# Batch 0 of a linear-attention and MLP kernel: k's sums as rows, two denominators at once, numerators of two chunks in single banks

## The chip, the core and the metric

The kernel runs on one core of a Trainium2 chip. The core has five engines that work side by side and meet at semaphores: PE (TensorE, matmuls and transposes, with PEld for its weight loads), DVE (VectorE), ACT (ScalarE), POOL (GpSimd) and SP (SyncE, which here only starts transfers). Each engine takes its instructions strictly in the order in which the program gives them. Matmul results land in PSUM, which PE writes and VectorE and ScalarE read; a bank of it holds 512 fp32 values in each of 128 partitions. The metric is the device time of one launch in microseconds, as the median of several runs.

## What is computed

Linear attention with cosine weights, then a two-layer MLP, in fp32 at the borders:

```python
def phi(x, c, s):                      # c, s: cos and sin of pi/2 * position / S
    r = np.maximum(x, 0.0)
    return np.concatenate([r * c, r * s], axis=-1)
q_p, k_p = phi(q, cos_w, sin_w), phi(k, cos_w, sin_w)
kv  = np.einsum('bhsf,bhsd->bhfd', k_p, v)
z   = np.sum(k_p, axis=2)
num = np.einsum('bhsf,bhfd->bhsd', q_p, kv)
den = np.einsum('bhsf,bhf->bhs', q_p, z)[..., None] + 1e-06
x   = (num / den), heads side by side  # [B*S, H*D]
h   = x @ w_in
out = (h * (1.0 / (1.0 + np.exp(-1.702 * h)))) @ w_out
```

B = 8 batches, H = 8 heads, S = 576 positions, D = 64, so phi has 128 features; d_model = 512, d_ff = 2048.

## The kernel before, in words

Batches run one after the other. For each, k and q are turned into `kr` and `qn` (`trig`, L142 on VectorE or POOL and L140 on ScalarE), PE forms k^T v per pair of heads (`kv_mm`, L207), q is transposed into `qT` (features on partitions), numerators are `qT` times k^T v (`num_mm`, L230), VectorE divides them by the denominators (`num_div`, L254, after L236 and L238), the quotient `xn` is transposed into `x` (model dimension on partitions), and the MLP follows: `mm1` (L295) with its gelu on ScalarE (L300), `mm2` (L332) with its copy out (L336). In steady state the attention of the next batch is spread between the matmuls of `mm2`. A batch has 576 positions: four chunks of 128 and a tail of 64, and the tails of all batches go through the MLP together at the end (L312).

The order on every engine is written out by hand: the calls at the end of the kernel are the program order, there is no scheduler that moves them. Waits are put in where one engine reads what another writes, and where a buffer is used again. Two pools in PSUM matter. `pmm` has four buffers of one bank (named `mm`), `pat` two buffers of two banks (named `at`). A buffer is given out again in turn, and its next writer waits for the last reader of the tile before.

Batch 0 has nothing to hide behind, and its order (L355 to L435) is what the change touches:

- SP issues k in two parts (chunks 0 to 2, then 3 to 8, in pieces of 64 positions) and q in two parts (0 to 3, 4 to 8). POOL waits for k's first part through a one-element copy into `gate` (L130) and then issues v in two halves of two head pairs (`vb`) and the column groups 0 and 1 of W_in. After its own share of q (piece 8, L142) and a second `gate` copy that waits for v's second half (L383), it issues groups 2 and 3, and then the loads for batch 1 and W_out.
- PE begins with filler matmuls on a zeroed tile (`idle`, L346), then sums k over positions: `ksum` (L218) takes `kr` as the weights and a two-column selector `sel` as the moving operand, four matmuls of two columns for each of nine pieces, with one filler between pieces. The result has features on partitions, so VectorE copies it straight into column 64 of `kvs` (`ksum_evac`, L222). `kvs` holds k^T v and z side by side.
- `qturn_pe(c)` (L171) transposes the two 64-position pieces of chunk c, and `qevac(c)` copies them into `qT` (L181 on VectorE, L179 on ScalarE).
- `kv_mm(0, 2)` and `kv_mm(2, 4)` form k^T v for the two halves of the head pairs, `kv_evac` (L212) copies them into `kvs`.
- `den_early(0)` (L244) forms the denominators of chunk 0 alone, ahead of its numerators. For chunks 1 to 4 the denominator is column 64 of each head's numerator block, so `num_mm` writes 65 columns per head into a two-bank tile of `pat`.
- `xturn_mm(c)` (L274) transposes `xn` into columns of the same `pat` tile that the numerators leave free, `xturn_evac` (L280, ScalarE) copies it into x. The tail goes by a transposing transfer on SP (`xturn_dma`, L285).
- `part(c, fcs)` runs `mm1` for one chunk and one or more column blocks `fc` of W_in: four matmuls of 128 columns each (`mm1_part`, L295). The four blocks 0 to 3 are filled chunk by chunk in four banks, and then `gelu` runs on them and `mm1(0, 4)` begins, with 512 columns at a time.

Of the kernel before, what the change touches and what calls it, by code (L numbers as in the profile page):

```python
# [9 lines left out]
F32 = mybir.dt.float32  # L10
BF16 = mybir.dt.bfloat16
# [8 lines left out]
def kernel(  # L20
# [9 lines left out]
    nc = tc.nc  # L30
# [30 lines left out]
    for t, src, cut in ((kf, k, 192), (qf0, q, 256)):  # L61
# [10 lines left out]
    nc.gpsimd.memset(ident, 1.0)  # L72
    nc.gpsimd.affine_select(out=ident, in_=ident, compare_op=mybir.AluOpType.is_equal,
                            fill=0.0, base=0, pattern=[[-1, 128]], channel_multiplier=1)
    warm = const.tile([128, 512], BF16)
    nc.vector.memset(warm, 0.0)
    pos_f = const.tile([128, NP], F32)
    nc.vector.tensor_copy(pos_f, pos_i)
    nc.vector.tensor_scalar(pos_f[64:128, 0:NS], pos_f[64:128, 0:NS], float(-S), None, op0=ADD)
# [43 lines left out]
    def load_win(g):  # L123
        nc.gpsimd.dma_start(out=w_in_sb[g], in_=win_r[:, :, ts(g, 512)])
# [10 lines left out]
    def trig(dst, src, j, act=False, eng=nc.vector):  # L135
        i = src[:, :, ts(j, 64)]
        for cs, w in enumerate((cosw, sinw)):
            o = dst[:, j, :, ts(cs, 64)]
            if act:
                nc.scalar.activation(o, i, AF.Relu, scale=w[:, j:j + 1])  # L140
            else:
                eng.tensor_scalar(o, i, 0.0, w[:, j:j + 1], op0=MAX, op1=MUL)  # L142
# [21 lines left out]

    tps = {}

    def qturn_pe(c, home=None):
        tp = pmm.tile([128, 2, NI, 128], BF16, name="mm") if home is None else home
        for j in range(2 * c, min(2 * c + 2, NS)):
            for i in range(NI):  # L170
                nc.tensor.transpose(tp[:, j % 2, i], qn0[:, j, i, :], ident)  # L171
        tps[c] = tp

    def qevac(c, act=False):
        n = min(2 * c + 2, NS) - 2 * c
# [26 lines left out]
    def kv_mm(i0, i1, rhs, col, n):  # L202
        for i in range(i0, i1):
            for j in range(NS):
                for hh in range(2):
                    r = slice(hh * 64, hh * 64 + 64)
                    nc.tensor.matmul(st["kv", i][:, hh, ds(col, n)], kr[r, j, i, :], rhs(r, i, j),  # L207
                                     start=(j == 0), stop=(j == NS - 1))

    def kv_evac(i0, i1, n=65):  # L210
        o = st["kvs"][:, :, i0:i1, 0:n]
        nc.vector.tensor_copy(o, st["ps", i0].rearrange("p hh (i e) -> p hh i e", e=65)[:, :, :, 0:n])  # L212

    def ksum(j):
        if j == 0:
            st["z"] = pmm.tile([128, NI, 2], F32, name="mm")
        for i in range(NI):
            nc.tensor.matmul(st["z"][:, i], kr[:, j, i, :], sel, start=(j == 0 and i == 0),  # L218
                             stop=(j == NS - 1 and i == NI - 1))

    def ksum_evac():
        nc.vector.tensor_copy(st["kvs"][:, :, :, 64], st["z"].rearrange("f i hh -> f hh i"))  # L222
# [11 lines left out]
    def inv_of(d):  # L234
        den = small.tile([128, 2, 4], F32, name="den")
        nc.vector.tensor_scalar(den, d, 1e-6, None, op0=ADD)  # L236
        inv = small.tile([128, 2, 4], F32, name="inv")
        nc.vector.reciprocal(inv, den)  # L238
        return inv

    def den_early(c):
        d = pmm.tile([128, 2, 4], F32, name="mm")
        for h in range(H):
            nc.tensor.matmul(d[:, h // 4, h % 4:h % 4 + 1], qT[:, h, ts(c, 128)],  # L244
                             st["kvs"][:, h % 2, h // 2, 64:65], start=True, stop=True)
        return inv_of(d)

    def num_div(c, inv=None):
        ps = nums[c][0]
# [13 lines left out]
    def x_open(b):  # L263
        x[b] = xpool.tile([128, KC, MT], BF16, name="xT")
# [74 lines left out]
                eng = nc.sync if last else nc.gpsimd  # L339
                eng.dma_start(out=dst[:, c0:c1], in_=ysb[p0:p0 + n, c0:c1])  # L340

    def idle(n, w=None):
        if w is None:
            w = pmm.tile([128, 512], F32, name="mm")
        for _ in range(n):
            nc.tensor.matmul(w, warm[:, 0:128], warm, start=True, stop=True)  # L346
        return w

    def vb_rhs(r, i, j):
# [2 lines left out]
    def vt_rhs(r, i, j):  # L352
        return vt[r, j, i, 0:65]

    w = idle(12)  # L355
    for j in (0, 1):
        trig(kr, kf, j)
    for j in (2, 6, 7, 8):
# [2 lines left out]
        trig(kr, kf, j)  # L361
    kv_open(0, 2)
    kv_open(2, 4)
    for j in (0, 1, 2):
        ksum(j)
    for j in (3, 6, 4, 7, 5):
        idle(1, w)
        ksum(j)
    idle(1, w)
    ksum(8)  # L370
    for j in (0, 1):
        trig(qn0, qf0, j)
    ksum_evac()
    idle(1, w)
    qturn_pe(0)
    for j in (2, 3):
        trig(qn0, qf0, j, act=True)
    idle(2, w)
    qturn_pe(1)
    for j in (4, 5):  # L380
        trig(qn0, qf0, j)
    trig(qn0, qf0, 8, eng=nc.gpsimd)
    nc.gpsimd.tensor_copy(gate[0:1, 1:2], vb[0:1, 3, 0:1])  # L383
    load_win(2)
    load_win(3)
    kv_mm(0, 2, vb_rhs, 0, 64)
    qturn_pe(2)
    for j in (6, 7):
        trig(qn0, qf0, j, act=True)
    qevac(0)  # L390
    qevac(1)
    qevac(2, act=True)
    inv0 = den_early(0)
    kv_evac(0, 2, 64)
    kv_mm(2, 4, vb_rhs, 0, 64)
    kv_evac(2, 4, 64)
    qturn_pe(3)
    qevac(3, act=True)
    num_mm(0)
    num_div(0, inv0)  # L400
    num_mm(1)
    num_div(1)
    qturn_pe(4)
    qevac(4)
    idle(1)
    x_open(0)
    xturn_mm(0)
    xturn_evac(0, 0)
    num_mm(2)
    num_div(2)  # L410
    xturn_mm(1)
    xturn_evac(0, 1)

    def part(c, *fcs):
        for fc in fcs:
            mm1_part(0, fc, c * 128, c * 128 + 128)

    part(0, 0, 1, 2, 3)
    num_mm(3)
    num_div(3)  # L420
    xturn_mm(2)
    xturn_evac(0, 2)
    part(1, 0, 1, 2, 3)
    num_mm(4)
    num_div(4)
    xturn_mm(3)
    xturn_evac(0, 3)
    xturn_dma(0, 4)
    part(2, 0, 1, 2)
    part(3, 0, 1)  # L430
    part(2, 3)
    part(3, 2, 3)
# [150 lines left out]
```

## Time and profile before

| what | us |
|---|---|
| median of 3 runs | 291.59 (291.50 to 292.52) |
| the profiled execution | 292.75 |
| its span, first to last instruction | 291.0 |
| k's second part: first use on VectorE | 6.79 |
| q's second part: first use on VectorE | 10.67 |
| first matmul of k^T v | 11.38 |
| first matmul of W_in (chunk 0) | 16.97 |
| busy: PE, ACT, DVE, POOL | 281.8, 133.1, 123.7, 37.8 |

All times of instructions are from the profiled execution, counted from the start of its span. A group of the profile is a source line, an engine, an operation and its tiles; `PE at L230` in the chain of waits is a matmul of line 230 that writes a tile named `at`. In the timeline, a bracket behind a row tells how long the engine was idle before it and what ended that. Matmul rows are longer than the distance between their starts, because matmuls overlap in the array; where a sum goes by distances of starts, the text says so. Some matmul records are missing from a trace.

### The profile page before, as it was taken

How to read it: one execution, taken by the hardware profiler on the slowest of the kernel's cores; microseconds unless marked ns; L12 is line 12 of the kernel's file. 1: busy time of each engine (PE TensorE's matmuls, PEld its weight loads, DVE VectorE, ACT ScalarE, POOL GpSimd, SP SyncE). 2: the span in 40 equal slices, each digit the busy share in tenths (PEclk: the TensorE clock that was granted, in tenths of full speed). 3: DMA queues.
4: the chain of work that ended last, by engine and by line, in shares of the span. 5: the costliest groups of instructions: out<-in, count | busy, mean ns of one | idle time of the engine just before them, and what ended most of it. 6: DMA issues, size and time to landing. Idle time of an engine off the chain costs nothing.

```text
span 291.0 us, 5656 instructions
## 1 busy us (share of the span) xinstructions
PE 281.8 (97%) x2247; PEld 153.0 (53%) x2282; DVE 123.7 (43%) x356; ACT 133.1 (46%) x232; POOL 37.8 (13%) x71
## 2 busy tenths in 40 slices
PE   6989999999999999999999999999999999999995
PEld 2685475555555555555455545554555455544444
DVE  3872656912657354826582567156624200000000
ACT  6857564793157214721463136412651176751111
POOL 6560042301210011001100110011000100002000
PEclk9999999999999999999999999999999999999999
DMA  7999999982699877989797579846952600002322
GB/s 239 247 213 289 368 247 362 239 193 76 128 271 260 219 131 260 289 184 147 221 314 198 96 203 346 222 102 159 373 94 72 119 36 1 0 2 44 84 90 72
DMA packets 67770, 52.48 MB, mean 180 GB/s; under 512 B 47968, under 2 KB 57952, under 8 KB 67744
## 3 DMA queue, kind: packets, MB, share of 16 engines
q1 hardware_dynamic: 60320, 32.52, 47.0%
q0 software_dynamic: 7424, 19.60, 23.9%
q8 instruction: 18, 0.29, 0.4%
q14 instruction: 8, 0.07, 0.1%
HBM read 36.70 MB, written 9.44 MB: 159 GB/s over the span
## 4 chain that ended last, share of the span: by engine, by line
PE 91%; DMA 3%; ACT 2%; DVE 1%; issue 1%; SPq 1%; ACTq 0%
PE mm L332 42%; PE mm L295 37%; PE mm L312 5%; PE at L230 3%; PE at L207 3%; DMA qf<-in_q_dram 3%; ACT g L300 1%; PE at L274 1%; DVE qn L142 1%; DVE qT L181 0%; PE at L171 0%; ACT qT L179 0%; SPq L62 0%; DVE xn L254 0%; ACT xT L280 0%
## 5 line engine op out<-in xcount | busy, mean ns | idle before, releaser
L332 PE MATMUL mm<-w_out_sb,g 128*128 128x512 bf16 (+1 forms) x506 | 116.7, 372 | 1.3 <-issue 0.2
L295 PE MATMUL mm<-xT,w_in 128*128 128x512 bf16 (+1 forms) x551 | 111.9, 360 | 0.5
L300 ACT ACTIVATE g<-mm 128x512 bf16<-128x512 f32 x128 | 75.6, 598 | 31.0 <-PE mm L295 31.0
L295 PEld LDWEIGHTS <-w_in 128*128 128x128 bf16 x560 | 59.8, 113 | 50.9
L332 PEld LDWEIGHTS <-g 128*128 128x128 bf16 x528 | 48.6, 98 | 49.1
L336 ACT ACTIVATE ysb<-mm 128x512 f32<-128x512 f32 (+1 forms) x37 | 21.7, 586 | 105.9 <-PE mm L332 103.0
L340 POOL DMA_DIRECT2D out_dram<-ysb x39 | 21.3, 547 | 204.7 <-ACT ysb L336 204.7
L142 DVE TENSOR_SCALAR kr<-kf,cosw 128x256 bf16<-128x256 f32 x64 | 22.6, 353 | 29.4 <-DMA kf<-in_k_dram 29.4
L254 DVE TENSOR_TENSOR xn<-at,inv 128x512 bf16<-128x512 f32 x40 | 27.7, 691 | 1.9 <-PE at L230 0.4
L142 DVE TENSOR_SCALAR kr<-kf,sinw 128x256 bf16<-128x256 f32 x64 | 22.2, 347 | 0.0
L212 DVE CAST kvs<-at 128x520 bf16<-128x520 f32 (+1 forms) x9 | 5.6, 634 | 33.7 <-PE at L207 33.7
L236 DVE TENSOR_SCALAR den<-at 128x8 f32<-128x8 f32 x39 | 6.5, 166 | 31.4 <-PE at L230 31.4
L230 PEld LDWEIGHTS <-qT 128*128 128x128 bf16 x320 | 14.8, 97 | 8.8 <-issue 0.8
L230 PE MATMUL at<-kvs,qT 128*128 128x65 bf16 x320 | 16.1, 193 | 0.7 <-ACT xT L280 0.7
L155 DVE TENSOR_SCALAR qn<-qf,sinw 128x512 bf16<-128x512 f32 (+1 forms) x30 | 14.4, 480 | 0.0
L155 DVE TENSOR_SCALAR qn<-qf,cosw 128x512 bf16<-128x512 f32 (+1 forms) x30 | 14.3, 476 | 0.0
L312 PE MATMUL mm<-xt,w_in 128*128 128x512 bf16 x63 | 13.9, 379 | 0.1
L332 PE MATMUL mm<-w_out_sb,gl_t 128*128 128x512 bf16 x63 | 13.9, 379 | 0.1
L313 ACT ACTIVATE gl_t<-mm 128x512 bf16<-128x512 f32 x16 | 9.6, 597 | 4.2 <-PE mm L312 4.2
L207 PEld LDWEIGHTS <-kr 64*128 64x128 bf16 x576 | 9.3, 94 | 2.8 <-issue 2.5
L312 PEld LDWEIGHTS <-w_in 128*128 128x128 bf16 x64 | 7.2, 113 | 6.6
L332 PEld LDWEIGHTS <-gl_t 128*128 128x128 bf16 x64 | 6.3, 98 | 7.5
(63 smaller groups left out, 114.5 us busy)
## 6 DMA issues: line engine op xcount, KB each, us to landing
kf<-in_k_dram SPq DMA_DIRECT2D x5, 1152.0 KB, 6.7
vf<-in_v_dram SPq DMA_DIRECT2D x5, 1152.0 KB, 9.5
qf<-in_q_dram SPq DMA_DIRECT2D x5, 1024.0 KB, 5.9
out_dram<-ysb POOLq DMA_DIRECT2D x20, 256.0 KB, 3.9
out_dram<-ysb POOLq DMA_DIRECT2D x19, 128.0 KB, 3.2
kf<-in_k_dram POOLq DMA_DIRECT2D x2, 1152.0 KB, 11.3
vf<-in_v_dram POOLq DMA_DIRECT2D x2, 1152.0 KB, 15.7
w_in<-in_moe_w_in_dram POOLq DMA_DIRECT2D x4, 512.0 KB, 9.5
```

The lines of the kernel that those rows point to most:

```text
L142: eng.tensor_scalar(o, i, 0.0, w[:, j:j + 1], op0=MAX, op1=MUL)
L155: nc.vector.tensor_scalar(o, i, 0.0, sc, op0=MAX, op1=MUL)
L207: nc.tensor.matmul(st["kv", i][:, hh, ds(col, n)], kr[r, j, i, :], rhs(r, i, j), start=(j == 0), stop=(j == NS - 1))
L230: nc.tensor.matmul(ps[:, h // 4, ds((h % 4) * 65, 65)], qT[:, h, ts(c, 128)], st["kvs"][:, hh, i, 0:65], start=True, stop=True)
L254: nc.vector.tensor_tensor(xn, pv[:, :, :, 0:64], inv.unsqueeze(3).to_broadcast([128, 2, 4, 64]), op=MUL)
L295: nc.tensor.matmul(hp[fc][:, t0:t1], w_in_of(kc, fc), x[b][:, kc, t0:t1], start=(kc == 0), stop=(kc == KC - 1))
L300: nc.scalar.activation(g, hp.pop(fc), AF.Gelu_apprx_sigmoid)
L312: nc.tensor.matmul(hps, w_in_of(kc, fc), xt[:, kc, :], start=(kc == 0), stop=(kc == KC - 1))
L313: nc.scalar.activation(gl_t[:, fc, :], hps, AF.Gelu_apprx_sigmoid)
L332: nc.tensor.matmul(yp[t, c0][:, c0:c1], w, w_out_sb[:, fc, c0:c1], start=(fc == 0), stop=(fc == FC - 1))
L336: nc.scalar.activation(ysb[:, c0:c1], yp[t, c0][:, c0:c1], AF.Identity)
L340: eng.dma_start(out=dst[:, c0:c1], in_=ysb[p0:p0 + n, c0:c1])
```

## The change

The numbers of lines in the profile shift: of the functions named here, `idle` becomes L380, `ksum` L218, `ksum_turn` L227, `qturn_pe` L173, `den_early` L253 with L256 and L258, `num1_mm` L264, `num1_div` L269, `x1turn_mm` L276, `x1turn_evac` L280, `num_mm` L238, `xturn_mm` L308, `mm1_part` L329.

- k's sums: `sel` becomes the weights (two columns) and `kr` the moving operand, so a piece takes one matmul of 512 columns, and the sum of all nine lies as a row per half of the partitions in two partitions. ScalarE copies the rows to SBUF in bf16 (`ksum_row`), four tiny matmuls turn them (`ksum_turn`), and VectorE copies the result into `kvs` as before, but behind the first `kv_evac`.
- Fillers: three in fp32 ahead of k in place of twelve in bf16, none between the k sums, where six stood, two further on in place of three (one each ahead of `qturn_pe(0)` and `qturn_pe(1)`), none ahead of `x_open`.
- `den_early(2)` forms the denominators of chunks 0 and 1 in one tile, with one sum and one reciprocal on VectorE.
- `num1_mm` writes the numerators of chunks 0 and 1 with 64 columns per head into one bank each, out of `pmm`; the transposed quotient goes back into the same bank.
- Order: `qturn_pe(3)` is split in two around `kv_mm(2, 4)` and `den_early`; the numerators of both chunks stand side by side, `num_mm(2)` ahead of the first turn of x, `num_mm(3)` and `qturn_pe(4)` between the first two. The copy of q's last piece moves from VectorE to ScalarE. The parts of `mm1` are cut finer: two blocks of chunk 0, two of chunk 1, and so on.

```diff
@@ -72,8 +72,9 @@
     nc.gpsimd.memset(ident, 1.0)
     nc.gpsimd.affine_select(out=ident, in_=ident, compare_op=mybir.AluOpType.is_equal,
                             fill=0.0, base=0, pattern=[[-1, 128]], channel_multiplier=1)
-    warm = const.tile([128, 512], BF16)
-    nc.vector.memset(warm, 0.0)
+    warm32 = const.tile([128, 128], F32)
+    nc.vector.memset(warm32, 0.0)
+    warm = warm32.bitcast(BF16)
     pos_f = const.tile([128, NP], F32)
     nc.vector.tensor_copy(pos_f, pos_i)
     nc.vector.tensor_scalar(pos_f[64:128, 0:NS], pos_f[64:128, 0:NS], float(-S), None, op0=ADD)
@@ -164,12 +165,12 @@
 
     tps = {}
 
-    def qturn_pe(c, home=None):
-        tp = pmm.tile([128, 2, NI, 128], BF16, name="mm") if home is None else home
-        for j in range(2 * c, min(2 * c + 2, NS)):
+    def qturn_pe(c, home=None, js=(0, 1)):
+        if js[0] == 0:
+            tps[c] = pmm.tile([128, 2, NI, 128], BF16, name="mm") if home is None else home
+        for j in range(2 * c + js[0], min(2 * c + js[-1] + 1, NS)):
             for i in range(NI):
-                nc.tensor.transpose(tp[:, j % 2, i], qn0[:, j, i, :], ident)
-        tps[c] = tp
+                nc.tensor.transpose(tps[c][:, j % 2, i], qn0[:, j, i, :], ident)
 
     def qevac(c, act=False):
         n = min(2 * c + 2, NS) - 2 * c
@@ -211,12 +212,19 @@
         o = st["kvs"][:, :, i0:i1, 0:n]
         nc.vector.tensor_copy(o, st["ps", i0].rearrange("p hh (i e) -> p hh i e", e=65)[:, :, :, 0:n])
 
-    def ksum(j):
-        if j == 0:
-            st["z"] = pmm.tile([128, NI, 2], F32, name="mm")
+    def ksum(j, first=False, last=False):
+        if first:
+            st["zr"] = pmm.tile([128, 512], F32, name="mm")
+        nc.tensor.matmul(st["zr"][0:2], sel, kr[:, j].rearrange("p i f -> p (i f)"), start=first, stop=last)
+
+    def ksum_row():
+        st["zrow"] = small.tile([2, 512], BF16, name="zrow", bufs=1)
+        nc.scalar.activation(st["zrow"], st["zr"][0:2], AF.Copy)
+
+    def ksum_turn():
+        st["z"] = pmm.tile([128, NI, 2], F32, name="mm")
         for i in range(NI):
-            nc.tensor.matmul(st["z"][:, i], kr[:, j, i, :], sel, start=(j == 0 and i == 0),
-                             stop=(j == NS - 1 and i == NI - 1))
+            nc.tensor.matmul(st["z"][:, i], st["zrow"][:, ts(i, 128)], ident[0:2, 0:2], start=True, stop=True)
 
     def ksum_evac():
         nc.vector.tensor_copy(st["kvs"][:, :, :, 64], st["z"].rearrange("f i hh -> f hh i"))
@@ -238,12 +246,38 @@
         nc.vector.reciprocal(inv, den)
         return inv
 
-    def den_early(c):
-        d = pmm.tile([128, 2, 4], F32, name="mm")
+    def den_early(n):
+        ps = pmm.tile([128, n, 2, 4], F32, name="mm")
+        for c in range(n):
+            for h in range(H):
+                nc.tensor.matmul(ps[:, c, h // 4, h % 4:h % 4 + 1], qT[:, h, ts(c, 128)],
+                                 st["kvs"][:, h % 2, h // 2, 64:65], start=True, stop=True)
+        den = small.tile([128, n, 2, 4], F32, name="den2", bufs=1)
+        nc.vector.tensor_scalar(den, ps, 1e-6, None, op0=ADD)
+        inv = small.tile([128, n, 2, 4], F32, name="inv2", bufs=1)
+        nc.vector.reciprocal(inv, den)
+        return inv
+
+    def num1_mm(c):
+        st["n", c] = pmm.tile([128, 512], F32, name="mm")
         for h in range(H):
-            nc.tensor.matmul(d[:, h // 4, h % 4:h % 4 + 1], qT[:, h, ts(c, 128)],
-                             st["kvs"][:, h % 2, h // 2, 64:65], start=True, stop=True)
-        return inv_of(d)
+            nc.tensor.matmul(st["n", c][:, ts(h, 64)], qT[:, h, ts(c, 128)],
+                             st["kvs"][:, h % 2, h // 2, 0:64], start=True, stop=True)
+
+    def num1_div(c, inv):
+        xn = small.tile([128, 2, 4, 64], BF16, name="xn", bufs=4)
+        nc.vector.tensor_tensor(xn, st["n", c].rearrange("p (a h e) -> p a h e", a=2, h=4),
+                                inv.unsqueeze(3).to_broadcast([128, 2, 4, 64]), op=MUL)
+        nums[c] = xn
+
+    def x1turn_mm(c):
+        xv = nums.pop(c).rearrange("p a h e -> p (a h e)")
+        for kc in range(KC):
+            nc.tensor.transpose(st["n", c][:, ts(kc, 64)].bitcast(BF16), xv[:, ts(kc, 128)], ident)
+
+    def x1turn_evac(b, c):
+        i = st["n", c][:, 0:256].bitcast(BF16).rearrange("p (k t) -> p k t", k=KC)
+        nc.scalar.activation(x_of(b, c), i, AF.Copy)
 
     def num_div(c, inv=None):
         ps = nums[c][0]
@@ -339,11 +373,12 @@
                 eng = nc.sync if last else nc.gpsimd
                 eng.dma_start(out=dst[:, c0:c1], in_=ysb[p0:p0 + n, c0:c1])
 
-    def idle(n, w=None):
+    def idle(n, w=None, t=warm):
         if w is None:
             w = pmm.tile([128, 512], F32, name="mm")
         for _ in range(n):
-            nc.tensor.matmul(w, warm[:, 0:128], warm, start=True, stop=True)
+            nc.tensor.matmul(w, t[:, 0:128], t[:, 0:128].unsqueeze(1).to_broadcast([128, 4, 128]),
+                             start=True, stop=True)
         return w
 
     def vb_rhs(r, i, j):
@@ -352,7 +387,7 @@
     def vt_rhs(r, i, j):
         return vt[r, j, i, 0:65]
 
-    w = idle(12)
+    w = idle(3, t=warm32)
     for j in (0, 1):
         trig(kr, kf, j)
     for j in (2, 6, 7, 8):
@@ -361,72 +396,74 @@
         trig(kr, kf, j)
     kv_open(0, 2)
     kv_open(2, 4)
-    for j in (0, 1, 2):
-        ksum(j)
-    for j in (3, 6, 4, 7, 5):
-        idle(1, w)
-        ksum(j)
-    idle(1, w)
-    ksum(8)
+    order = (0, 1, 2, 3, 6, 4, 7, 5, 8)
+    for j in order:
+        ksum(j, j == order[0], j == order[-1])
     for j in (0, 1):
-        trig(qn0, qf0, j)
-    ksum_evac()
-    idle(1, w)
-    qturn_pe(0)
-    for j in (2, 3):
-        trig(qn0, qf0, j, act=True)
-    idle(2, w)
-    qturn_pe(1)
-    for j in (4, 5):
         trig(qn0, qf0, j)
     trig(qn0, qf0, 8, eng=nc.gpsimd)
     nc.gpsimd.tensor_copy(gate[0:1, 1:2], vb[0:1, 3, 0:1])
     load_win(2)
     load_win(3)
+    idle(1, w)
+    qturn_pe(0)
+    for j in (2, 3):
+        trig(qn0, qf0, j, act=True)
+    ksum_row()
+    for j in (4, 5):
+        trig(qn0, qf0, j)
+    idle(1, w)
+    qturn_pe(1)
     kv_mm(0, 2, vb_rhs, 0, 64)
-    qturn_pe(2)
     for j in (6, 7):
         trig(qn0, qf0, j, act=True)
+    ksum_turn()
+    qturn_pe(2)
     qevac(0)
     qevac(1)
+    kv_evac(0, 2, 64)
+    ksum_evac()
     qevac(2, act=True)
-    inv0 = den_early(0)
-    kv_evac(0, 2, 64)
+    qturn_pe(3, js=(0,))
     kv_mm(2, 4, vb_rhs, 0, 64)
     kv_evac(2, 4, 64)
-    qturn_pe(3)
+    inv01 = den_early(2)
+    qturn_pe(3, js=(1,))
     qevac(3, act=True)
-    num_mm(0)
-    num_div(0, inv0)
-    num_mm(1)
-    num_div(1)
-    qturn_pe(4)
-    qevac(4)
-    idle(1)
-    x_open(0)
-    xturn_mm(0)
-    xturn_evac(0, 0)
+    num1_mm(0)
+    num1_mm(1)
+    num1_div(0, inv01[:, 0])
+    num1_div(1, inv01[:, 1])
     num_mm(2)
     num_div(2)
-    xturn_mm(1)
-    xturn_evac(0, 1)
+    x_open(0)
+    x1turn_mm(0)
+    x1turn_evac(0, 0)
+    qturn_pe(4)
+    num_mm(3)
+    num_div(3)
+    x1turn_mm(1)
+    x1turn_evac(0, 1)
+    qevac(4, act=True)
 
     def part(c, *fcs):
         for fc in fcs:
             mm1_part(0, fc, c * 128, c * 128 + 128)
 
-    part(0, 0, 1, 2, 3)
-    num_mm(3)
-    num_div(3)
+    part(0, 0, 1)
+    part(1, 0, 1)
+    part(0, 2)
     xturn_mm(2)
     xturn_evac(0, 2)
-    part(1, 0, 1, 2, 3)
+    part(0, 3)
+    part(1, 2, 3)
+    part(2, 0, 1)
+    xturn_mm(3)
+    xturn_evac(0, 3)
     num_mm(4)
     num_div(4)
-    xturn_mm(3)
-    xturn_evac(0, 3)
     xturn_dma(0, 4)
-    part(2, 0, 1, 2)
+    part(2, 2)
     part(3, 0, 1)
     part(2, 3)
     part(3, 2, 3)
```

## The prediction

> **What bounds the kernel now.** I read the page first, then the chain of waits in order of time, then PE's timeline of the first 23 us, then the waits of each engine.
>
> ```profile
> PE 281.8 (97%) x2247; PEld 153.0 (53%) x2282; DVE 123.7 (43%) x356; ACT 133.1 (46%) x232; POOL 37.8 (13%) x71
> ```
>
> PE is busy for 97% of the span, and the waits of PE behind 22 us sum to 0.2 us. So behind 22 us only PE's work counts, and the change leaves that as it is. What it can win lies in batch 0, whose end I take as the start of the first 512-column matmul of `mm1(0, 4)`, at 21.69 us (the last 128-column matmul starts at 21.635 and takes its place for 0.056). The result is the shift of that start.
>
> The chain of waits in order of time (start, length, what) says what batch 0 waits for:
>
> ```profile
> 2.39 8.26 DMA qf<-in_q_dram
> 10.64 0.03 issue
> 10.67 1.51 DVE qn L142 x4
> 12.18 0.60 DVE qT L181
> 12.79 0.05 issue
> 12.83 0.35 PE mm L244 x8
> ...
> 14.68 0.70 DVE xn L254
> 15.38 0.05 issue
> 15.42 0.41 PE at L274 x4
> 15.84 0.02 issue
> 15.86 0.61 ACT xT L280
> 16.46 0.04 issue
> 16.51 0.40 PE at L230 x8
> 16.91 0.22 PE at L274 x4
> 17.13 0.89 PE mm L295 x16
> ```
>
> Until 16.5 PE is not the limit: q's second part lands at 10.64, then VectorE makes qn, qT and the division, then ScalarE makes x. From 16.51 PE runs on. PE's timeline shows the two pauses of that passage in brackets:
>
> ```profile
> 15.42 0.40 PE L274 MATMUL at<-ident,xn 128*128 128x128 bf16 x4 [0.32 <-DVE xn L254]
> 16.51 0.40 PE L230 MATMUL at<-kvs,qT 128*128 128x65 bf16 x8 [0.69 <-ACT xT L280]
> 16.97 1.06 PE L295 MATMUL mm<-xT,w_in 128*128 128x128 bf16 x16
> ```
>
> The second pause is a buffer: `num_mm(2)` needs the two-bank tile that `xturn_evac(0)` is still reading.
>
> **Units, all from this trace.** PE starts per matmul, from the distance of starts: 512 columns 0.216, 128 columns or a transpose 0.056, 64 or 65 columns 0.029, one column 0.025. From the start of a last transpose to the copy that waits for it 0.256 (15.60 to 15.86); for a numerator 0.23 (16.715 to 16.945). From an engine's end to the PE instruction that waits for it 0.05 to 0.06. ScalarE's copy of x 0.60, of qT 1.02. VectorE: qT copy 0.67, kvs copy 0.37, z copy 0.20, sum with 1e-6 to reciprocal 0.19, reciprocal to division 0.24, division 0.69, the next instruction 0.08 ahead of an end.
>
> **Part 1: ahead of k^T v.** Removed: 36 one-pass k sums (36 x 0.025 = 0.9 us), 12 + 10 bf16 fillers. Added: 3 fp32 fillers, 2 bf16 ones, 9 row sums of 512 columns (9 x 0.216 = 1.9 us). All of it lies beside transfers: `kv_mm(0, 2)` starts at 11.38 because v's first half was issued at 4.50 and took 6.8, so it is there at 11.3. The row sums follow k (last kr on ScalarE 9.29): the last ends at 9.57, the filler at 9.78, `qturn_pe(0)` is done at 10.23, `qturn_pe(1)` waits for ScalarE's qn until 10.94 as now. Worth 0. The fp32 filler has no row: if one costs a bf16 one (0.43 at the start) the three end at 2.5; if they cost what the twelve did, at 5.3. I take 5.3, the same memory swept; up to 7.4, when the fourth k chunk comes, neither end moves anything. POOL keeps its order (q's chunk 8, gate, `load_win(2)`, `load_win(3)`, kf), so the transfers start as now.
>
> **Part 2: z by way of a row.** `ksum_row` is a new ScalarE copy of 2x512 between q's chunks 3 and 6. Bounds: 0.21 (128x14, L89) to 0.60 (128x512); I take 0.60, as many elements in each partition. It puts chunks 6 and 7 and the copy of qT's chunk 2 off by 0.5 (12.48 to 13.0 for the last qn), and behind it waits `ksum_turn`, four transposes of 0.03 on PE at 12.0. Cover: PE needs chunk 7 only at 14.25 and qT's chunk 2 only at 14.94. Cost 0; without that cover 0.5.
>
> **Part 3: the chain on VectorE.** qT copies as now, 12.10 to 13.37; `kv_evac(0, 2)` 13.30 to 13.67; `ksum_evac` 13.59 to 13.78, which now stands here (it was at 9.64, beside a wait); `kv_evac(2, 4)` follows PE and is not late. `den_early` for two chunks starts when z is there, 13.84: 16 x 0.025, last start 14.22. Sum at 14.42 (128x16 has no row; 0.15 of 128x8 to 0.35 of 128x256, I take 0.15), reciprocal 14.61, inverse at 14.81. PE: chunk 7 turned to 14.47, `num1_mm(0)` to 14.70. First division 14.91 to 15.60, second 15.52 to 16.21. Now they run 14.68 to 15.37 and 15.71 to 16.40. **The first is 0.23 late, the second 0.19 early**: z and the double denominators stand ahead of the first, while the second loses its own sum and reciprocal.
>
> **Part 4: PE and ScalarE to the end of batch 0.** `x1turn_mm(0)` 15.66, ScalarE 16.09 to 16.69, first part of W_in at 16.74 (now 16.97). PE meanwhile does `qturn_pe(4)` and `num_mm(3)` to 16.35, `x1turn_mm(1)` to 16.57; ScalarE 16.78 to 17.37. What is left on PE at 16.74 is 64 x 0.056 + two transposed chunks 0.45 + `num_mm(4)` 0.24 = 4.26, without stalls 21.0. Stalls, from the order of the calls:
> - `part(0,0,1)` ends at 17.19, x of chunk 1 is there at 17.42: 0.23.
> - Between `xturn_mm(2)` and its reader lie 12 matmuls (0.67); the trip by ScalarE takes 0.85 (0.20 + 0.60 + 0.05): 0.18.
> - Between `xturn_mm(3)` and its reader lie `num_mm(4)` and 4 matmuls (0.46) against the same 0.85: 0.39.
>
> 21.0 + 0.80 = 21.80. Now: 21.69. The buffer wait of 0.69 is gone, and three waits for x take its place, because only two or three short parts stand between a turn and its reader where now whole chunks of 16 matmuls (0.89) do. Sum: **+0.1 us**. The w_in transfers are no bound: group 0 is there at 6.15 + 9.1 = 15.3, group 1 (6.90 + 11.8) at 18.7. `xturn_dma(0, 4)` leaves SP some 0.6 later (20.86 to 21.5), lands in about 9.7, and is read only by the tails (L312) behind 250 us; SP's next transposes come behind 50 us. The gelu of the first group starts near 21.1 and gives its buffer 0.05 ahead of need.
>
> If batch 0 ends earlier, q of batch 1 could become the limit: it lands at 34.8, its last qn on VectorE is at 37.6, and PE turns it at 38.09. That is 1.5 us of room for the second pair of chunks, more than any gain below needs.
>
> The profiled execution took 292.75 with a span of 291.0, so 1.75 around it; it stands 1.16 above the median of the three runs (291.59, 291.50 to 292.52). With +0.1 it would read 292.85; the median 291.7.
>
> **The rivals.**
>
> *The stalls close* (faster). For: xn of chunk 1 is early, the banks are PE's own, and each stall depends on a trip of 0.85 against fillers that I add from starts. If all three close, the end is 21.0, -0.7: 290.9. Against: ScalarE's own 0.60 is in each trip, and 0.60 + 0.05 is already above 0.46. Chance 0.25.
>
> *The early chain itself is shorter* by 0.8 more, so that the gain passes 0.5% (1.46 us): it needs the divisions at 14.2, ahead of the z copy on VectorE that follows 1.27 us of qT copies behind q's landing. Chance 0.04; 290.0.
>
> *PE's clock falls back* (slower). Place: PE between 6.4 and 16. The fillers of 512 columns start 0.43 apart until 4.20 and 0.216 after, though the granted clock reads 1.00 in every slice: PE begins at half speed and was at full after 2.95 us of work. The change takes 8 full fillers away and puts in sums that fill two columns of the array; if PE slows again and the slow stretch (2.95 us, as at the start) falls on 16.7 to 19.7, it does half its work there: +1.5, 293.1. It decides when transposes start 0.11 apart instead of 0.056. Against: the row sums keep PE running for the same 1.9 us, the longest pause now is 1.05 (before 7.46) and harmed nothing. Chance 0.10.
> The Trainium skill, "TensorE: Matmul & The Clock Gate", Part 1, says that the clock is gated by recent activity and drops after an idle window; its Part 4 says that transposes are not counted as activity, which speaks against this change. The trace agrees on the start at half speed; that transposes starve the clock no row here shows (they run at 0.056 behind the fillers).
>
> *The change does nothing where it says* is half of my forecast: what stands ahead of k^T v waits for v anyway.
>
> **Numbers.** Forecast 0.61 (own range 291.2 to 292.2: -0.4 to +0.5 for the three stalls and the unknown rows), stalls closed 0.25, clock 0.10, shorter chain 0.04. A change of 0.5% (1.46 us) is about what a measurement of this kernel can tell from none. Faster by more: 0.04; within: 0.61 + 0.25 = 0.86; slower by more: 0.10. The range takes in the forecast, the closed stalls and the scatter of the runs upward (0.9 over the median), and leaves 0.14 out: 290.6 to 292.8.
>
> **What would show it.** In the changed profile: `kv_mm(0, 2)` still at 11.4; den near 14.4, the divisions near 14.9 and 15.5; the first L329 matmul near 16.7; three pauses of PE before 21 ended by ScalarE's xT; `mm1(0, 4)` near 21.8. Wrong it is if the pauses are absent, if the divisions start ahead of 14.6, or if transposes are spaced 0.11.

## The result and the profile after

The changed kernel takes 292.28 us (median of 22 runs, 291.98 to 293.99) against 291.63 for the kernel before (22 runs, 291.46 to 292.52). The ratio is 1.0021, 95% interval 1.0011 to 1.0030: slower by 0.3 to 0.9 us, and within the 0.5% that the prediction named as no change, though the interval, 0.1% to either side, is narrower than that. The profiled execution took 292.39 with a span of 290.7.

The engines' busy times hardly moved; this is the first part of the page of the changed kernel:

```profile
PE 283.2 (97%) x2220; PEld 152.8 (53%) x2253; DVE 123.1 (42%) x353; ACT 134.1 (46%) x234; POOL 37.7 (13%) x71
```

The chain of waits in order of time (start, length, what) tells where batch 0 spends itself now:

```profile
2.39 7.33 DMA qf<-in_q_dram
9.72 0.03 issue
9.75 1.51 DVE qn L143 x4
11.26 0.60 DVE qT L182
11.86 0.04 issue
11.90 0.83 PE mm L173 x12
12.73 0.64 PE at L208 x36
13.37 0.50 PE mm L253 x16
13.87 0.02 issue
13.89 0.19 DVE den L256
14.08 0.02 issue
14.11 0.26 DVE inv L258
...
14.46 0.70 DVE xn L269
15.16 0.05 issue
15.21 0.40 PE mm L276 x4
```

Before, the chain went from the copy of qT to the denominators. Now the copy of qT (`qevac(0)`, 11.26 to 11.86) releases transposes on PE (`qturn_pe(2)`, L173), and behind them stand `kv_mm(2, 4)` (L208) and the denominators (L253). PE's timeline of the same execution shows the pause, and further on those that the prediction named:

```profile
10.74 0.71 PE L208 MATMUL at<-vb,kr 64*128 64x64 bf16 x36
11.38 0.25 PE L227 MATMUL mm<-ident,zrow 2*128 2x2 bf16 x4
11.90 0.83 PE L173 MATMUL mm<-ident,qn 128*128 128x128 bf16 x12 [0.28 <-DVE qT L182]
12.67 0.71 PE L208 MATMUL at<-vb,kr 64*128 64x64 bf16 x36
13.31 0.55 PE L253 MATMUL mm<-kvs,qT 128*128 128x1 bf16 x16
...
16.29 1.52 PE L329 MATMUL mm<-xT,w_in 128*128 128x128 bf16 x20
17.65 0.39 PE L308 MATMUL at<-ident,xn 128*128 128x128 bf16 x4
17.87 1.46 PE L329 MATMUL mm<-xT,w_in 128*128 128x128 bf16 x20
19.16 0.39 PE L308 MATMUL at<-ident,xn 128*128 128x128 bf16 x4
19.39 0.41 PE L238 MATMUL at<-kvs,qT 128*128 128x65 bf16 x8
19.63 0.39 PE L329 MATMUL mm<-xT,w_in 128*128 128x128 bf16 x4
20.23 2.14 PE L329 MATMUL mm<-xT,w_in 128*128 128x128 bf16 x23 [0.21 <-ACT xT L314]
```

Only the last of the three pauses carries a bracket; the other two lie inside the rows of 20, as a distance of starts of 0.30 at 16.68 and of 0.23 at 18.49 (the third is 0.43, at 19.80).

**How two executions are compared.** From the start of the first 512-column matmul of `mm1(0, 4)` to the end of the span it is 269.3 to 269.5 us in the profile of every kernel of this study: the whole effect lies in batch 0, as the prediction took it. But transfers land at other times in each execution (q's second part between 9.29 and 10.64, v's first half between 10.62 and 11.61), and the execution on which the prediction rests was a late one. So I compare distances between starts:

| distance, us | before | after |
|---|---|---|
| `kv_mm(0, 2)` to `kv_mm(2, 4)` | 1.39 (second profile of before), 1.74 (q late) | 1.93 (1.60 without the pause of PE) |
| `kv_mm(2, 4)` to the first division | 1.56 | 1.79 |
| first division to first part of W_in | 2.29 | 1.83 |
| first part of W_in to `mm1(0, 4)` | 4.72 | 5.06 |
| the last three together | 8.57 | 8.68 |

The last three together differ by 0.11. The first row costs 0.2 more, through the four tiny matmuls of `ksum_turn`, and up to 0.33 more for the pause. The last three rows of before are from its first profile; in its second one W_in landed late and made the third row 2.66. Two profiles of before and one of after are too few to tell whether the transfers land, on the average, at the same times in both kernels: a share of the difference from there is not excluded.

### The profile page after: what moved, and what is told of

The parts are those of the page before. It is cut to its first block, busy times and chain, and to the rows that moved or that the text cites. A ratio compares the mean times of both kernels' runs of the same rounds, so it can differ in the third digit from the quotient of the medians.

```text
span 290.7 us, 5600 instructions
## 1 busy us (share of the span) xinstructions
PE 283.2 (97%) x2220; PEld 152.8 (53%) x2253; DVE 123.1 (42%) x353; ACT 134.1 (46%) x234; POOL 37.7 (13%) x71
## 4 chain that ended last, share of the span: by engine, by line
PE 91%; DMA 3%; ACT 2%; DVE 1%; issue 1%; SPq 1%; ACTq 0%; DVEq 0%
PE mm L366 42%; PE mm L329 37%; PE mm L346 5%; PE at L208 3%; PE at L238 3%; DMA qf<-in_q_dram 3%; ACT g L334 1%; DVE qn L143 1%; PE at L308 0%; DVE qT L182 0%; PE at L173 0%; PE mm L173 0%; ACT qT L180 0%; SPq L62 0%; DVE xn L269 0%
## 5 line engine op out<-in xcount | busy, mean ns | idle before, releaser
L329 PE MATMUL mm<-xT,w_in 128*128 128x512 bf16 (+1 forms) x551 | 112.3, 360 | 0.8 <-ACT xT L314 0.2
L329 PEld LDWEIGHTS <-w_in 128*128 128x128 bf16 x560 | 60.0, 113 | 51.5 <-issue 0.5
L288 DVE TENSOR_TENSOR xn<-at,inv 128x512 bf16<-128x512 f32 x38 | 26.3, 691 | 1.3
L238 PEld LDWEIGHTS <-qT 128*128 128x128 bf16 x304 | 14.1, 97 | 8.0
L238 PE MATMUL at<-kvs,qT 128*128 128x65 bf16 x304 | 15.4, 193 | 0.0
L208 PEld LDWEIGHTS <-kr 64*128 64x128 bf16 x576 | 9.3, 94 | 2.8 <-issue 2.5
```

Of the source, the lines that this page charges most:

```text
L238: nc.tensor.matmul(ps[:, h // 4, ds((h % 4) * 65, 65)], qT[:, h, ts(c, 128)], st["kvs"][:, hh, i, 0:65], start=True, stop=True)
L288: nc.vector.tensor_tensor(xn, pv[:, :, :, 0:64], inv.unsqueeze(3).to_broadcast([128, 2, 4, 64]), op=MUL)
L329: nc.tensor.matmul(hp[fc][:, t0:t1], w_in_of(kc, fc), x[b][:, kc, t0:t1], start=(kc == 0), stop=(kc == KC - 1))
```

## The experiments

All ratios are to the kernel before on the same chip. Theory A: the bank that z takes, and the three waits for x. Theory B: the row sums or the clock. Theory C: PE runs out of fetched instructions. Theories D and E come with the ninth run.

**z in a bank that is there already** (against the changed kernel):

```diff
-        st["z"] = pmm.tile([128, NI, 2], F32, name="mm")
+        st["z"] = st["zr"][:, 0:2 * NI].rearrange("p (i hh) -> p i hh", i=NI)
```

> The changed kernel, with one edit: ksum_turn writes z into the bank that already holds the row sums, so that it takes no buffer of its own. The wait of qturn_pe(2) for the qT copy of chunk 0 (0.38 us of pause at 11.9 in the changed kernel's trace) then goes to qturn_pe(3), which comes 0.45 later. Theory A (that wait delays kv_mm(2, 4), den_early and both divisions by 0.4, and three waits of PE for x cost 0.8 of what the rest wins): k^T v's second half 0.4 nearer to k^T v's first, divisions 0.35 nearer to q's landing (from 4.7 to 4.35), time against the kernel before +0.65 - 0.4 = +0.25. Theory B (the row sums and the fp32 fillers cost, by PE's clock or by ScalarE's 0.5): divisions and time as in the changed kernel, +0.65.

Measured: 292.35 against 291.92, ratio 1.0015 (1.0006 to 1.0024). The pause at 11.9 is gone and the first distance falls from 1.93 to 1.60:

```profile
10.85 0.71 PE L208 MATMUL at<-vb,kr 64*128 64x64 bf16 x36
11.49 0.25 PE L227 MATMUL mm<-ident,zrow 2*128 2x2 bf16 x4
11.67 0.84 PE L173 MATMUL mm<-ident,qn 128*128 128x128 bf16 x12
12.44 0.71 PE L208 MATMUL at<-vb,kr 64*128 64x64 bf16 x36
```

The transposes start at 11.67, while the copy of qT for chunk 0 still runs until 11.82: they no longer wait for it. By the ratios the time falls by 0.2 and not by 0.4, and the intervals do not part it from the changed kernel. A reason can be read from the traces: the pause is there only if the copy of qT starts more than some 0.2 behind `kv_mm(0, 2)`. It started 0.44 behind in the profile of the changed kernel, and -0.1 to 0.3 in most of the others; so in many executions nothing waits for the bank.

**The turns of x earlier** (against the changed kernel; `...` are the calls of chunk 3 up to `xturn_dma`):

```diff
     part(0, 0, 1)
+    xturn_mm(2)
+    xturn_evac(0, 2)
     part(1, 0, 1)
     part(0, 2)
-    xturn_mm(2)
-    xturn_evac(0, 2)
+    xturn_mm(3)
...
+    xturn_dma(0, 4)
     part(0, 3)
     part(1, 2, 3)
     part(2, 0, 1)
-    xturn_mm(3)
...
-    xturn_dma(0, 4)
     part(2, 2)
```

> The changed kernel, with xturn_mm(2) moved ahead of part(1, 0, 1) and xturn_mm(3) with num_mm(4) ahead of part(0, 3): the trips through ScalarE then have more matmuls beside them. Theory A: the pauses of 0.24, 0.18 and 0.38 before x of chunks 1, 2 and 3 shrink to 0.2 in all, the first 512-column matmul comes 0.55 nearer to q's landing (from 11.6 to 11.05), time against the kernel before +0.1. Theory B: PE waits for something else then, the time stays at +0.65.

Measured: 291.68, ratio 0.9993 (0.9984 to 1.0002): 0.8 below the changed kernel's ratio. The distance from the first part of W_in to `mm1(0, 4)` falls from 5.06 to 4.52. So the waits for x are real. The trace shows 0.53 less, with 0.24 of waiting left, now ahead of the turns of x (0.11 at 17.06 and 0.13 at 18.10 of that profile); by the ratios the time falls by 0.8, with 0.4 to either side, which takes in the 0.53.

**Both of these edits together.**

> Both edits: z in the bank of the row sums, and the early turns. Theory A: they add, 0.4 + 0.55: the first 512-column matmul 10.7 behind q's landing, time against the kernel before -0.3. Theory B: between the changed kernel and the better of the two single edits, not below the kernel before.

Measured: 291.59, ratio 0.9990 (0.9981 to 0.9999), 0.3 faster than the kernel before. No other kernel of the study lies below the time before with its whole interval.

**The rest of the change without the rows**: before's `ksum`, its fillers and its early `ksum_evac`, the rest as changed.

```diff
-    w = idle(3, t=warm32)
+    w = idle(12)
...
-    for j in order:
-        ksum(j, j == order[0], j == order[-1])
+    for j in (0, 1, 2):
+        ksum(j)
+    for j in (3, 6, 4, 7, 5):
+        idle(1, w)
+        ksum(j)
+    idle(1, w)
+    ksum(8)
```

> The changed kernel with the k sums and fillers of the kernel before (36 matmuls of two columns, 22 bf16 fillers, z copied at 9.6, no copy of a row on ScalarE): only the single banks, the double denominators and the new order are left. Theory A: z takes a bank early, the wait of qturn_pe(2) goes as in the first edit, time +0.2 to +0.3; the rows as such cost nothing. Theory B: the rows were all of the loss, time 0.0 or below.

Measured: 292.42, ratio 1.0019 (1.0010 to 1.0028). The first distance is 1.42, as Theory A wants, but a new pause stands in PE's timeline, in the middle of a part of W_in:

```profile
15.81 0.33 PE L321 MATMUL mm<-xT,w_in 128*128 128x128 bf16 x3
16.75 1.11 PE L321 MATMUL mm<-xT,w_in 128*128 128x128 bf16 x17 [0.61 <-issue]
```

"issue" as the releaser means that nothing in the profile released PE: the matmul needs the same x, the same weights' transfer and the same bank as the three before it, which ran. The queue that carries instructions (`q8 instruction` among the DMA queues) began a transfer of 16 KB at 14.45, 2.29 us earlier. That was Theory C, formed here.

**The kernel before once more, for a second profile.**

> The kernel before, unchanged, for a second profile. In its first one q's second part and v's halves landed 0.6 to 0.9 us later than in the profiles of the changed kernel and the four edits (10.65 against 9.3 to 9.8; v's first half 11.34 against 10.6 to 11.2), which start their loads with the same instructions at the same times. Theory: that is scatter between executions; here q lands at 9.3 to 9.9, and the first 512-column matmul is again 10.9 to 11.3 behind it, at about 20.8 instead of 21.69. If the old way of summing k delays the transfers, q lands near 10.6 again.

Measured: one run of 292.36 with a span of 290.7. q landed at 9.52 and `kv_mm(2, 4)` came 1.39 behind `kv_mm(0, 2)`. `mm1(0, 4)` began at 21.23, later than expected, because group 0 of W_in landed only at 16.44; PE waited 0.20 for it.

**The rows alone**: the kernel before with the row sums and the few fillers, `ksum_evac` between the two copies of qT.

```diff
+    ksum_turn()
     qturn_pe(2)
     qevac(0)
+    ksum_evac()
     qevac(1)
```

> The kernel before with the k sums as rows and the few fillers alone (z copied between the two qT copies on VectorE); denominators, numerators and parts stay as before. Theory A: qturn_pe(2) again waits for the qT copy of chunk 0, whose bank it takes, which puts kv_mm(2, 4) 0.4 to 0.5 later and the first division with it: time against the kernel before +0.4. If the rows cost nothing: 0.0.

Measured: 291.96 against 291.76, ratio 1.0018 (1.0006 to 1.0029). The medians differ by 0.2 and the ratio says 0.5: seven of the twelve runs lie between 291.79 and 292.01, the other five between 292.51 and 293.16. The distance of the two `kv_mm` is 1.58 instead of 1.39, the rest of batch 0 as before.

**Neither rows nor the fillers between the sums.**

```diff
-    order = (0, 1, 2, 3, 6, 4, 7, 5, 8)
-    for j in order:
-        ksum(j, j == order[0], j == order[-1])
+    for j in (0, 1, 2, 3, 6, 4, 7, 5, 8):
+        ksum(j)
```

> The edit without rows, with the changed kernel's few fillers (3 in fp32, 2 in bf16) in place of 22 bf16 ones: 37 PE instructions fewer ahead of batch 0's main work. In the edit without rows PE stood still for 0.83 us in the middle of part(0, 0), at its 450th instruction, with no semaphore to wait for, 2.3 us after a 16 KB transfer of instructions began. Theory C (PE ran out of fetched instructions): the pause goes, the wait for x of chunk 1 (0.24) comes back, time 0.4 below the edit without rows, +0.1 against the kernel before. If the pause was something else (W_in's landing, a buffer) it stays, +0.5.

Measured: 292.90, ratio 1.0042 (1.0030 to 1.0054). A miss, and a useful one. PE's busy time and granted clock by stretches (window, length, PE, PEld, DVE, ACT and POOL busy with instructions, then the granted clock, DMA share, GB/s):

```profile
6.00:8.00 2.00, 1.39 (x29) 0.93 (x27) 1.85 (x6) 1.85 (x5) 1.55 (x2) 1.00 1.07 389
8.00:10.00 2.00, 1.71 (x23) 1.10 (x23) 1.97 (x8) 2.00 (x6) 0.47 (x1) 0.88 1.18 270
10.00:12.00 2.00, 2.00 (x45) 1.72 (x43) 2.00 (x5) 1.84 (x5) 1.86 (x2) 0.50 1.21 205
12.00:14.00 2.00, 2.00 (x58) 1.84 (x55) 0.52 (x3) 0.92 (x1) 1.94 (x4) 0.76 1.25 209
14.00:16.00 2.00, 1.60 (x49) 1.48 (x47) 1.81 (x5) 1.13 (x2) 2.00 (x4) 1.00 1.24 208
```

The granted clock falls to 0.50. Worked out from 0.88, 0.50 and 0.76 the half speed lasts 0.48 + 2.00 + 0.96 = 3.4 us, and it falls on the transposes of q and on k^T v:

```profile
10.92 1.16 PE L208 MATMUL at<-vb,kr 64*128 64x64 bf16 x36
12.01 1.27 PE L173 MATMUL mm<-ident,qn 128*128 128x128 bf16 x12
```

The same rows take 0.71 and 0.83 after the change. The two `kv_mm` stand 2.29 apart, 0.9 more than the 1.42 of the run without rows, which has the fillers. The pause for instructions is gone, as Theory C wants (5.06 from the first part of W_in to `mm1(0, 4)`), but the clock costs more than that gains. The rival of the falling clock is thus a real mechanism of this kernel. The Trainium skill, "TensorE: Matmul & The Clock Gate", Part 1, has a warm-up budget of about 3.4 us at half rate; the stretch here agrees. Its Part 4, by which transposes do not count as busy in the same way as other matmuls, would fit too: between 6.3 and 8.8 us this kernel ran column sums of two columns, then one filler and, from 9.04 on, transposes, and the trace's clock falls at 9.53; no run here parts the two.

**More instructions ahead of W_in** (against the run with both): fifty one-column matmuls in place of one fp32 filler, all of them long done before v lands.

```diff
-    w = idle(3, t=warm32)
+    w = idle(2, t=warm32)
+    for _ in range(50):
+        nc.tensor.matmul(w[:, 0:1], warm[:, 0:128], warm[:, 0:1], start=True, stop=True)
```

> The version with both edits, with 50 one-column matmuls (100 PE instructions) in place of one of the three fp32 fillers, all of them while PE waits for k. The work behind them is the same. Theory C: PE reaches the end of its fetched instructions ahead of the fetch, a pause of 0.5 to 1.2 us without a semaphore appears between 14 and 17, time 0.4 to 0.9 above the version with both edits. If instruction fetch is no limit: the same as that version, -0.3.

Measured: 292.67, ratio 1.0032 (1.0021 to 1.0043), 1.2 above the run with both. PE's timeline of it:

```profile
16.25 0.23 PE L238 MATMUL at<-kvs,qT 128*128 128x65 bf16 x2
17.50 0.34 PE L238 MATMUL at<-kvs,qT 128*128 128x65 bf16 x6 [1.03 <-issue]
```

Here the pause cuts through the eight matmuls of one `num_mm(3)`. It ends at 17.50, and the 16 KB of instructions began to move at 15.21: 2.29 again. The distance from `kv_mm(0, 2)` to `mm1(0, 4)` is 10.78 against 9.75, 1.03 more, which is the pause. Theory C holds. The 14 kept traces say more. In the five whose PE pauses without a semaphore (this one, the run without rows, and three runs further on) the first matmul behind the pause is the 224th that the trace holds (the 223rd in the run without rows), be it a part of W_in, a numerator or a transpose. In the other nine the 224th comes 2.32 to 3.45 us behind the start of the same transfer, and there is no such pause. So a pause comes when PE reaches that point of its program ahead of the instructions. The Trainium skill, "Runtime: NRT & Kernel Launch", Instruction fetch mechanics, has instructions refilled in blocks of 16 KiB and the crossing as mostly hidden; the size agrees, and here the crossing is not hidden.

**The changed kernel without any filler.**

```diff
-    w = idle(3, t=warm32)
...
-    idle(1, w)
...
-    idle(1, w)
```

> The changed kernel without a single filler matmul: nothing runs on PE ahead of the row sums of k. It tells what kept PE's clock in the run with few fillers and column sums, where the granted clock read 0.7 in the slice from 7.3 to 14.6 us and transposes started 0.11 apart. Theory D (the nine 512-column row sums, 1.9 us of PE work that streams 512 columns each, are themselves enough to bring PE to full speed): transposes of q and k^T v at full speed, kv_mm(0, 2) to kv_mm(2, 4) 1.9 apart as in the changed kernel, time as the changed kernel, +0.1 to +0.5 over the time before. Rival E (the fillers are what brought it there; PE begins at half speed and needs some 3 us of work, which the row sums alone do not fill): granted clock below 0.9 in the second slice, transposes 0.11 apart, 36 matmuls of k^T v in 1.2 instead of 0.7, the divisions about 1 later, time +1.0 to +2.0 over before.

Measured: 292.44, ratio 1.0023 (1.0014 to 1.0032), as the changed kernel. Where the row sums follow one another they start 0.38 to 0.43 apart, up to the last, and the first transposes up to 0.107; only from 10.2 us on do transposes start 0.056 apart. PE's timeline:

```profile
9.72 1.27 PE L173 MATMUL mm<-ident,qn 128*128 128x128 bf16 x16
10.92 0.71 PE L208 MATMUL at<-vb,kr 64*128 64x64 bf16 x36
```

The row sums thus bring PE to full speed by themselves, as Theory D has it, but later: the trace's record of the clock begins at 10.17 here and at 5.94 in the changed kernel, where the distances of starts fall. k^T v runs at full speed (0.71). `kv_mm(0, 2)` came 0.20 behind the landing of v, against 0.05 in the changed kernel, and the times do not part the two. Rival E's slow transposes show until 10.2, but not its cost, and the few fillers are not shown to do anything for the time of the changed kernel.

**The six fillers put back between column sums** (against the run with neither).

```diff
-    for j in (0, 1, 2, 3, 6, 4, 7, 5, 8):
-        ksum(j)
+    for j in (0, 1, 2):
+        ksum(j)
+    for j in (3, 6, 4, 7, 5):
+        idle(1, w)
+        ksum(j)
+    idle(1, w)
+    ksum(8)
```

> The run with few fillers and column sums of k, with one thing put back: the six bf16 fillers that stood between the sums before (the three fp32 ones at the start and two later stay). If the clock fell back there because nothing wide ran on PE between 6.3 and 8.8 us, it is at full speed again: transposes 0.056 apart, granted clock 1.00 in every slice, kv_mm(0, 2) to kv_mm(2, 4) 1.4 apart as in the run without rows, and the time falls from +1.14 over before to +0.3 to +0.6. If it was something else (the fp32 fillers at the start, or the few fillers further on), the half speed stays and with it +1.0 to +1.3.

Measured: 292.19, ratio 1.0008 (0.9998 to 1.0017), 1.0 below that run; granted clock 1.00, the two `kv_mm` 1.42 apart. By the ratios it is also 0.4 below the changed kernel, which has the rows, and 0.3 below the run without rows, which has twelve bf16 fillers at the start; in both cases the intervals overlap. Its pause for instructions costs 0.23 instead of 0.53.

**That, with the early turns** (moved as in the second experiment).

> The run with column sums of k, the six fillers between them and the few other fillers, with the turns of x of chunks 2 and 3 moved ahead as in the run with early turns. If the two effects found so far are independent (rows cost 0.4, the three waits for x 0.8, all in batch 0), the time is that of the run before it (ratio 1.0008) less 0.8: ratio 0.998, -0.5 to -0.7 against the time before, and below the run with early turns and z in the fillers' bank (0.9990). If they are not independent (PE gets to the matmuls of W_in sooner than its instructions are fetched, and stands still there with no semaphore behind it), part of it is lost: ratio 0.999 to 1.000, and a pause ended by nothing shows between the first division and the first 512-column matmul.

Measured: 291.77 against 291.89, ratio 0.9994 (0.9985 to 1.0003). By the ratios it gained 0.4 and not 0.8, with 0.3 to either side of each. The distance from `kv_mm(0, 2)` to `mm1(0, 4)` fell by 0.67, from 10.34 to 9.67, and a pause with no semaphore behind it remains, 0.10, which ends 2.26 behind the start of the instructions' transfer. Nor does leaving out the rows show a gain here: the kernel with early turns and rows has 0.9993.

**And with two fp32 fillers and two bf16 ones less.**

```diff
-    w = idle(3, t=warm32)
+    w = idle(1, t=warm32)
...
-    idle(1, w)
...
-    idle(1, w)
```

> The same with one fp32 filler at the start instead of three, and without the two bf16 fillers further on, so that PE has some ten instructions fewer ahead of the matmuls of W_in. If the few fillers are not needed for the clock (six between the sums are enough), the time is that of the run beside it or up to 0.2 better, with any pause for instructions gone. If they are needed, transposes start 0.11 apart, the granted clock is below 1 between 9 and 13 us, and the time is 0.7 to 1.1 above the run beside it.

Measured: 292.27, ratio 1.0015 (1.0004 to 1.0026), 0.6 above the run beside it. The expected sign of lost fillers is there for a while: transposes start 0.107 apart until 10.6 us and 0.056 from then on.

```profile
9.84 1.39 PE L173 MATMUL mm<-ident,qn 128*128 128x128 bf16 x16
11.16 0.71 PE L208 MATMUL at<-vb,kr 64*128 64x64 bf16 x36
```

Until then PE runs at half speed, in the sums too (a filler with its four sums takes 0.53 instead of 0.32), though the view's granted clock reads 1.00, as it does in the first 4 us of the kernel before: the trace's record of the clock begins only at 10.57. So k's sums end later and VectorE, which copies z ahead of q, waits:

```profile
10.02 0.19 DVE L223 CAST kvs<-mm 128x8 bf16<-128x8 f32 x1 [0.71 <-PE mm L219]
```

That copy started at 9.37 in the run beside it, and the copies of qT at 11.09 instead of 11.55. `kv_mm(0, 2)` began at 11.16, 0.47 behind the landing of v, against 0.04 in the run beside it; that is 0.43 of delay, most of the 0.6 if it stands in the other executions too. The profiled execution itself took 291.73; in it v had landed early (10.69 against 11.04). The others go up to 293.13, and why was not profiled. The pause for instructions is still there, 0.10, with PE resuming 2.28 behind the start of the transfer.

## Why the prediction came out as it did

The forecast was 291.7 with +0.1; measured is +0.65 (0.3 to 0.9). The time lies in the range, and the direction and most of the terms hold. The size does not: the measured shift is several times the forecast one, and the range took it in because it was wide enough for the scatter of the runs upward. One sign of being wrong came up to the letter, divisions ahead of 14.6 (14.46), but only because q landed 0.92 earlier than in the profile that the prediction read; from q's landing the first division came later than forecast, 4.73 against 4.27. Point by point:

- **What bounds the kernel** held: nothing behind `mm1(0, 4)` moved.
- **Part 1** held: `kv_mm(0, 2)` still waits for v. The fp32 fillers end at 6.26, later than the 2.5 to 5.3 that the prediction reckoned with and still ahead of the 7.4 up to which, it said, nothing moves.
- **Part 4** held to the hundredth: first division to first part of W_in 1.83 as forecast, from there to `mm1(0, 4)` 5.06 as forecast. The stalls of 0.23, 0.18 and 0.39 were measured as 0.24, 0.18 and 0.38 (distances of starts less 0.056), and the run with early turns shows that the time falls when most of that is removed. The rival *the stalls close* is refuted. One reading in this part was wrong without touching the sum: of the three waits for x not all are new. Before, 12 matmuls and not 16 stood between `xturn_mm(3)` and the reader of its x, and PE waited 0.18 there, up to 20.58, for ScalarE's copy, which ended at 20.52:

```profile
19.50 0.39 PE L274 MATMUL at<-ident,xn 128*128 128x128 bf16 x4
19.93 0.60 ACT L280 ACTIVATE xT<-at 128x512 bf16<-128x512 bf16 x1 [0.77 <-PE at L274]
```

- **The step that failed is Part 2's "Cost 0"**, with Part 3's "starts when z is there". z is there 3.20 behind q's landing, as forecast (forecast 13.84 with q at 10.64; measured 12.93 with q at 9.73). But `den_early` starts 0.38 later than that, because it stands on PE behind `kv_mm(2, 4)`, and this is late: between the two `kv_mm` PE has no slack once v has landed. I gave the new copy on ScalarE a cover and forgot the two things that z costs on PE: four matmuls (0.2), and a turn of the four `mm` banks. The new tile makes `qturn_pe(2)` wait for `qevac(0)`, 0.28 idle in this profile. Against q's landing the first division is 0.69 later than in the first profile of before (4.73 against 4.04), not 0.23; in the second profile of before it is 4.31, because there `kv_mm(0, 2)` waits for v, 1.34 behind q.
- **What that step cost.** The runs put the rows at 0.5 (rows alone, 1.0018) and 0.4 (column sums with six fillers, 1.0008 against 1.0021), but at nothing where the turns are early (0.9993 with rows, 0.9994 without). Each interval reaches 0.3 to either side. So that the chain is longer by 0.2 to 0.5 between the two `kv_mm` is shown by the traces. From the landing of v's first half to `mm1(0, 4)` it is 10.35 and 10.37 in the two profiles of before (10.00 in the second without the 0.37 that the late W_in adds), 10.17 with the rows alone, 10.33 with z in the bank of the row sums, and 10.66 in the changed kernel: 0.33 more than an undisturbed execution of before where the pause is absent, 0.66 where it stands. How many executions have the pause no run counts, so how much of the measured 0.65 comes from the tile stays open within these bounds.
- **The clock** stayed up once PE had come to full speed (5.94), as forecast, and for the reason given against the rival: the row sums keep PE at work. The run with neither rows nor fillers between the sums shows what it would have cost: 1.0, at 9.5 to 12.9 us, where the prediction had set 1.5 at 16.7 to 19.7.
- **What I had no term for** is the instruction fetch. The kernel before has no pause of that kind, and the changed one has none. Whoever keeps the fillers and moves only the rest meets it (0.53).

The buffer stall of 0.69 is gone, as the change has it, and brought nothing: waits for x of 0.80 in all, 0.62 of them new, and a later first division took its place; that was forecast. What is left on top of the forecast, about 0.5 in the median, lies where the rows lengthen the chain, with the reservation above.

## What to carry to other kernels

Ask of a moved or added tile not only who computes it but whose bank it takes in the rotation: the wait turns up at the next user, here a transpose that had nothing to do with z. Between a turn of data on PE and its reader put more work than the whole trip to the other engine and back; if parts are cut finer, move the turns forward with them. Filler matmuls are part of the design: before they are taken out, see what else streams wide operands in that stretch and when PE has to be at full speed; before they are added, count them against the instructions that PE must fetch.

## What the runs showed of the hardware

- PE can stand still in the middle of a group of like matmuls with no semaphore in the profile: 0.61 idle, 1.03, and as distances of starts 0.23, 0.10 and 0.10 more than usual. In these five PE resumed 2.21 to 2.29 us after a transfer of 16 KB began on the instruction queue, each time at the 223rd or 224th matmul of the trace. Which instruction starts the transfer stays open.
- Half speed of PE came back for 3.4 us after PE had been at full speed: for 2.5 us it had run nothing but two-column matmuls, and the fall came 0.7 us later, during transposes. Row sums of 512 columns with two columns of weights kept it at full speed, and without any filler brought it there, at 10.2 us.
- PE's half speed at the start does not show in the granted clock of the views, which reads 1.00 there: the trace's record of the clock begins at 4.18 in the kernel before, 5.94 in the changed one, 10.17 and 10.57 in two others, and there the distances of starts halve.
- An fp32 matmul of 512 columns appears as two rows. Their starts lie 0.85 us apart while PE is at half speed, where bf16 ones lie 0.43 apart, and 0.43 at full speed (run with both edits), where bf16 ones lie 0.216 apart: an fp32 matmul takes four times as long as one in bf16.
- From one execution to the next the landings of the first transfers scatter by 1.0 to 1.4 us, while the runs of a kernel lie mostly within 1 of each other: distances between starts told more than times of day.
